# New planning constants for the last five attention blocks, and a later bank for output tiles, in a planned attention-and-MLP kernel

## The chip, the cores and the metric

The kernel runs on one core of a Trainium2 chip. The metric is the device time of one execution in microseconds (us), as the median of several runs; lower is better.

## The reference

One layer over S = 2048 positions with D = 448 channels. The input is normalized, and an attention with 16 heads of 28 channels and a two-layer MLP of width 1792 both read the normalized input. The MLP's result, through a silu, is a gate on the attention's projected output:

```python
xn = _layernorm(x)                      # x: (1, 2048, 448)
q, k, v = heads(xn @ wqkv)              # 16 heads of 28
p = softmax(q @ k.T * 28 ** -0.5)       # (2048 x 2048) per head
s = merge(p @ v) @ wo
g = silu(gelu(xn @ w1 + b1) @ w2 + b2)  # w1: 448 x 1792
return x + s * g
```

## The kernel before

**Tiling.** The heads form four groups of four (G = 4), the queries four chunks of 512 (C = 4). A group and a chunk make a block, so there are 16 blocks, done in the order of `ORD`; the last five, numbers 11 to 15, are (3,0), (3,1), (3,2), (2,3) and (3,3). A block has 64 score tiles of 128 keys by 512 queries, numbered m, one per key tile and head. TensorE (PE) computes the scores into banks of PSUM (`ring`, and `misc`; line L1429), ScalarE (ACT) takes the exponential of two or three tiles in one instruction (L1485), and PE multiplies the result with the values into the bank `acc` (L1865).

**Late passes.** ACT is relieved of some tiles. `p_late` picks groups of four tiles (one key tile, four heads) and VectorE (DVE) makes a rough exponential of them by integer arithmetic: four instructions that read PSUM (L1714, one per tile) and two that add a shift over all four (L1773). The product with the values then takes three sets of matmuls instead of one, or two where GpSimd (POOL) first adds two of them (L1786, four instructions). Only eight key tiles of a block may be picked (four in block 15), and only those at least `QDIST` tiles ahead of the next score.

**A block's end.** `p_epi` copies the sums and products of the block out of PSUM on DVE (L1928), and sends the sums through a chain: a DMA to DRAM and one back (L1940, L1942; block 14 has four direct DMAs instead, L1937), a reciprocal on POOL (L1944), a DMA to DRAM (L1946), four DMAs that spread the reciprocals over the partitions (L1949), and a product on POOL (L1953), after which the block's heads are ready for the output projection. All DMAs of this chain are issued by SyncE (SP). Block 15 ends in four parts (`p_epi4`, `p_norm4`): a copy (L1897), a matmul that spreads the sums (L1909), a reciprocal on DVE or, in the last part, on ACT (L1916, L1913), a product on DVE (L1919).

**Output.** For a query chunk c there are four output tiles t. `p_out` (c = 0, 1, 2) and `p_last` (c = 3) take a bank, project with four matmuls (L1963), multiply with the gate (`t_oev`: L1980 on DVE; at the very end for c = 2 a copy on ACT, L1976, and a product on DVE, L1978), add x (L1984) and store (L1986 on SP); for c = 0 and 1 a DMA from POOL accumulates into the output (L1989). The gate itself comes from f2, the second MLP matmul (L1346, evicted by L1352), a tanh on ACT (L1362), and then two POOL instructions per tile (L1367, L1369) for c = 0 to 2. For c = 3 two DVE instructions (L1373) make three tiles, the first two of them and the third alone.

**What sets the order.** The program is written by a planner: `run` steps through generators, one for each piece of work, each of which yields a task with an engine, what it reads and writes, a duration and a rank; the planner keeps a clock for each engine, takes the task that can start first by its own costs, with ranks deciding among those that start within `EPS`, and appends it to that engine's instruction list. The chip then runs each engine's list in that order, with semaphores between the engines. A wrong duration thus changes no result; it makes an engine stand at an instruction whose input is not there yet, with everything behind it. A generator that needs a PSUM bank asks for it with a condition; `p_out` asks when `on_done` of its block is set, its gate is done, and the product L1953 lies in the planner's past. Constants in `BP` are one row for each block; `tune` loads the row when the scores reach the block. Among them are `OP`, the rank of output tiles (a low one goes first; scores have 1, and products with the values 1.01 to 6), `QDIST`, `QLEAD`, `ND4`, `LU`, `LQ`, `JMAX` and `DQ`, which set when late passes are picked and how many may be under way, `MG` (whether POOL adds), `R3` (whether ACT may take three tiles at once), and `EPS`, `MP`, `SLACK`, `UR`, which bend the choice on PE.

Of the kernel before, what the change touches and what calls it, by code (L numbers as in the profile page):

```python
# [18 lines left out]
G = 4  # L19
# [7 lines left out]
NBLK = G * C  # L27
# [23 lines left out]
)  # L51
NQ = (5, 11, 13, 13, 12, 7, 11, 10, 16, 3, 16, 15, 12, 13, 12, 14)
# [12 lines left out]
R3, OP = 0, 5.0  # L65
# [25 lines left out]
PVN = 2  # L91
OWN2 = 0
EA = 0
LNR = 1
G3P = 0
PATH = {(1, 2): 'D', (1, 3): 'D', (2, 0): 'D', (2, 1): 'D', (2, 2): 'D', (2, 3): 'D'}
# [30 lines left out]
class _Kernel:  # L127
# [1229 lines left out]
    def p_silu(self, c):  # L1357
        K = self
        yield ("until", lambda: K.f2n[c] == 4 and K.ready([K.b_fsb[c % 2]], 0.3) and (c < 2 or K.g_done[c - 2]))
        fb, sg = K.fsb[:, c % 2, :, :], K.sig[:, c % 2, :, :]  # L1360
        nt = 4 if c < C - 1 else 3
        yield _Task(ACT, lambda eng: eng.activation(sg[:, 0:nt, :], fb[:, 0:nt, :], ACTF.Tanh, scale=0.5),  # L1362
                    [K.b_fsb[c % 2]], [K.b_sig[c % 2]], 0.1 + 0.375 * nt, 0.0, 0)
        if c < C - 1:
            for t in range(nt):
                o = K.g_sb[:, c, t, :]
                yield _Task(POOL, lambda eng, o=o, t=t: eng.tensor_tensor(o, sg[:, t, :], fb[:, t, :], ALU.mult),  # L1367
                            [K.b_sig[c % 2], K.b_fsb[c % 2]], [K.b_h[c], K.b_g[c]], 1.05, 0.05, 3, port=True)
                yield _Task(POOL, lambda eng, o=o, t=t: eng.tensor_tensor(o, o, fb[:, t, :], ALU.add),  # L1369
                            [K.b_sig[c % 2], K.b_fsb[c % 2]], [K.b_h[c], K.b_g[c]], 1.05, 0.05, 3, port=True)  # L1370
        for t0 in range(0, nt if c == C - 1 else 0, 2):
            t1 = min(t0 + 2, nt)
            yield _Task(DVE, lambda eng, t0=t0, t1=t1: eng.scalar_tensor_tensor(  # L1373
                K.g_sb[:, c, t0:t1, :], sg[:, t0:t1, :], 1.0, fb[:, t0:t1, :], op0=ALU.add, op1=ALU.mult),
                        [K.b_sig[c % 2], K.b_fsb[c % 2]], [K.b_h[c], K.b_g[c]], 0.15 + 0.467 * (t1 - t0), 0.0, 3)
        K.g_done[c] = True
        if c == C - 2:
            K.b_x2[c].r = list(K.b_h[c].r) + [K.b_h[c].w]
            for y in K.b_h[1], K.b_h[2]:
                K.b_x2[c].r += y.r + [y.w]  # L1380
            xc = K.A_x[0].rearrange("(c p t) d -> c p t d", p=128, t=4)[c]
            for i in range(OWN2 // 2, 2):
                dst = K.h[:, 1 + i, 5632:5632 + 2 * D].rearrange("p (t d) -> p t d", d=D)
                K.dma(SP, lambda eng, i=i, dst=dst: eng.dma_start(dst, xc[:, 2 * i:2 * i + 2, :]), K.s_x3, writes=[K.b_x2[c]] if i else [])
        if c < C - 1:
            return
        K.b_x2[c].r = list(K.b_h[c].r) + [K.b_h[c].w]
        K.dma(SP, lambda eng: eng.dma_start(K.x2[1][:, :, :], K.A_x[0].rearrange("(c p t) d -> c p t d", p=128, t=4)[c]),
              K.s_x2[c], writes=[K.b_x2[c]])
        if nt < 4:  # L1390
            yield ("until", lambda: K.exp_m == MTOT - 1)
            o = K.g_sb[:, c, 3, :]
            yield _Task(ACT, lambda eng: eng.activation(sg[:, 3, :], fb[:, 3, :], ACTF.Tanh, scale=0.5),
                        [K.b_fsb[c % 2]], [K.b_sig3], 0.47, 0.0, 0)
            if LNR:
                K.prog[ACT].append(lambda eng: eng.preload_act_table_set("natural_log_exp_and_others"))
                K.tE[ACT] += 1.3
            E = POOL if G3P else DVE
            if not G3P:
                yield ("until", lambda: K.E_done == NBLK + 1)  # L1400
            yield _Task(E, lambda eng: eng.tensor_tensor(o, sg[:, 3, :], fb[:, 3, :], ALU.mult),
                        [K.b_sig3, K.b_fsb[c % 2]], [K.b_h[c], K.b_g3a], 1.05 if G3P else 0.39, 0.0, 2, port=E == POOL)
            if not G3P:
                yield ("until", lambda: K.on4[3])
            yield _Task(E, lambda eng: eng.tensor_tensor(o, o, fb[:, 3, :], ALU.add),
                        [K.b_fsb[c % 2], K.b_g3a], [K.b_h[c], K.b_g3], 1.05 if G3P else 0.39, 0.0, 2, port=E == POOL)
# [481 lines left out]
    def p_epi4(self, s):  # L1888
# [3 lines left out]
        yield ("until", lambda: K.on_done[NBLK - 3])  # L1892
        if s == 2 and EA:
            yield _Task(ACT, lambda eng: eng.activation(K.E_sb[:, 1, sl], K.acc[:, sl], ACTF.Copy), [K.b_acc],
# [9 lines left out]
    def p_norm4(self, t):  # L1904
# [6 lines left out]
        R = K.rf[:, t % 2, :]  # L1911
        if LNR and t == 3:
            yield _Task(ACT, lambda eng: eng.activation(R, bank[:, 0:128], ACTF.Ln), [tok], [K.b_rf[t % 2]], 0.25, 0.0, 0)  # L1913
# [9 lines left out]
    def p_epi(self, b):  # L1923
        K = self
        g, c = ORD[b]
# [3 lines left out]
        K.E_done = b  # L1929
        K.copying = False  # L1930
        yield ("until", lambda: K.late_on)
        lag = 2.2 if b >= NBLK - 4 else 4.0
        src = bass.AP(tensor=K.E_sb, offset=DH * 1024 + 512 * (b % 2), ap=[[32 * 1024, 4], [1, 512]])
        if b == NBLK - 2:
            for j in range(4):
# [57 lines left out]
    
    def p_out(self, c, t):
        K = self
        bank, tok = yield ("bank", lambda: K.pe_free() and K.on_done[11 + c] and K.g_done[c] and K.ready(K.b_onT[G - 1][c:c + 1]), lambda: OP)
        K.pe_wait += 1
        ps = bank[:, 0:D]
        yield K.t_wo(ps, tok, c, t, (0, 1), lambda: OP)
        yield K.t_wo(ps, tok, c, t, (2, 3), lambda: OP)  # L2000
        K.pe_wait -= 1
        yield from K.t_oev(ps, tok, c, t)
        K.banks.append((bank, tok))
# [63 lines left out]
```

## Time and profile before

| | |
|---|---|
| median of 3 runs | 421.41 us (421.1 to 421.66) |
| the profiled execution, whole | 421.52 us |
| its span in the profile | 419.7 us |
| ACT busy | 406.0 us, 97% |
| PE busy | 400.8 us, 95% |
| DVE busy | 344.6 us, 82% |
| POOL busy | 186.3 us, 44% |
| DMA queues | 15.29 MB moved, mean 36 GB/s |

The span is what the hardware profiler records on the core; 1.8 us of the execution lie outside it. A profile's busy time counts work and not waits between engines. PE's matmuls are pipelined and their ends are modelled, so PE's busy share is not its share of full speed. Ends of the last blocks, by the copy L1928: block 10 at 302.4 us, 11 at 325.9, 12 at 343.4, 13 at 370.8, 14 at 389.6; block 15's first part is copied (L1897) at 405.4 us.

### The profile page before, as it was taken

The page shows a single profiled execution, that of the slowest core. Times are in us where ns is not written, and L with a number is a line of the kernel's source. Part 1 is how long each engine was busy: PE and PEld are TensorE (multiplying, and loading weights), DVE is VectorE, ACT ScalarE, POOL GpSimd, SP SyncE. Part 2 cuts the span into 40 slices and gives each one's busy share as a digit, 9 for nine tenths or more (in the row PEclk, how much of TensorE's full clock was granted, in tenths as well). Part 3 has the DMA queues.
Part 4 walks back from the last instruction along what each step waited for, and adds up shares of the span by engine and source line. Part 5 has one row for each costly group of instructions (what it writes and reads, how often), then busy time and mean ns, then how long its engine had stood idle before and what let it go on. Part 6 is the DMA issues. An engine that isn't in the chain of part 4 may idle for free.

```text
span 419.7 us, 9637 instructions
## 1 busy us (share of the span) xinstructions
PE 400.8 (95%) x3664; PEld 133.1 (32%) x3664; DVE 344.6 (82%) x594; ACT 406.0 (97%) x415; POOL 186.3 (44%) x193
## 2 busy tenths in 40 slices
PE   6899999999999999999999999999999999999995
PEld 4443223332222222223223433232223223222452
DVE  8968899987785899999893126799996899898577
ACT  6999999999999999999999999999999999999995
POOL 7571333237769271212331514408246805921860
PEclk9999999999999999999999999999999999999998
DMA  8801000000001001000220000000000012320032
GB/s 264 269 2 39 3 14 15 20 11 16 24 2 27 2 1 29 2 27 15 83 89 26 27 1 2 2 2 22 7 1 28 3 28 52 47 41 28 3 91 92
DMA packets 15952, 15.29 MB, mean 36 GB/s; under 512 B 7129, under 2 KB 12993, under 8 KB 15874
## 3 DMA queue, kind: packets, MB, share of 16 engines
q1 hardware_dynamic: 15042, 13.07, 10.8%
q0 software_dynamic: 576, 0.92, 1.6%
q8 instruction: 29, 0.48, 0.5%
q10 hardware_dynamic: 288, 0.69, 0.4%
q14 instruction: 17, 0.14, 0.1%
HBM read 12.59 MB, written 2.93 MB: 37 GB/s over the span
## 4 chain that ended last, share of the span: by engine, by line
PE 71%; ACT 12%; DVE 8%; issue 6%; POOL 2%; ACTq 0%; DVEq 0%; POOLq 0%
PE ring L1429 22%; PE acc L1865 17%; PE ring L1277 9%; ACT P L1485 7%; PE ring L1346 4%; PE misc L1346 4%; PE ring L922 3%; ACT h L1485 3%; PE misc L922 3%; PE misc L1277 2%; PE misc L1216 2%; DVE vaug L1714 1%; ACT xnT L1485 1%; PE acc L1063 1%; PE ring L1216 1%
## 5 line engine op out<-in xcount | busy, mean ns | idle before, releaser
L1485 ACT ACTIVATE P<-ring 128x1024 bf16<-128x1024 f32 (+1 forms) x237 | 251.1, 1163 | 3.0 <-PE ring L1429 1.3
L1429 PE MATMUL ring<-qT,kT 32*128 32x512 bf16 (+2 forms) x1060 | 141.6, 357 | 7.8 <-ACT P L1485 2.1
L1485 ACT ACTIVATE h<-ring 128x1024 bf16<-128x1024 f32 (+1 forms) x80 | 87.3, 1194 | 0.1
L1429 PEld LDWEIGHTS ring<-qT,kT 32*128 32x128 bf16 x1060 | 38.1, 91 | 144.1 <-ACT P L1485 83.9
L1944 POOL TENSOR_TENSOR rc<-rs,mone 128x16 f32<-128x16 bf16 x15 | 45.0, 3002 | 30.9 <-DMA rs<-sums 23.0
L1865 PE MATMUL acc<-P,vaug 128*32 128x512 bf16 (+2 forms) x607 | 54.0, 353 | 0.0
L1277 PE MATMUL ring<-xnT,w 128*128 128x512 bf16 x180 | 48.9, 382 | 0.0
L1485 ACT ACTIVATE xnT<-ring 128x1024 bf16<-128x1024 f32 (+1 forms) x40 | 44.2, 1144 | 1.0 <-PE ring L1429 0.6
L1953 POOL TENSOR_TENSOR qT<-x_sb,E_sb 128x512 bf16<-128x512 f32 x15 | 18.5, 1234 | 47.4 <-DVE w L1773 14.1
L1429 PE MATMUL misc<-qT,kT 32*128 32x512 bf16 (+1 forms) x92 | 34.6, 379 | 0.0
L1346 PE MATMUL ring<-w,h 128*128 128x448 bf16 x126 | 30.8, 355 | 0.3 <-DVE vaug L1714 0.3
L1714 DVE TENSOR_SCALAR x_sb<-ring 128x512 uint16<-128x512 f32 x43 | 29.0, 686 | 1.7 <-PE ring L1429 1.3
L1171 POOL TENSOR_TENSOR qsq<-qT 128x512 bf16<-128x512 bf16 x12 | 12.5, 1040 | 34.0 <-DVE qT L1165 31.4
L1865 PE MATMUL acc<-h,vaug 128*32 128x512 bf16 (+1 forms) x226 | 27.2, 380 | 0.0
L1714 DVE TENSOR_SCALAR x_sb<-misc 128x512 uint16<-128x512 f32 x29 | 19.9, 687 | 8.1 <-PE misc L1429 7.4
L1346 PE MATMUL misc<-w,h 128*128 128x448 bf16 x98 | 24.3, 356 | 0.0
L1277 PEld LDWEIGHTS ring<-xnT,w 128*128 128x128 bf16 x180 | 14.7, 97 | 23.9 <-issue 8.3
L1714 DVE TENSOR_SCALAR h<-ring 128x512 uint16<-128x512 f32 x31 | 21.1, 686 | 0.3 <-PE ring L1429 0.2
L1367 POOL TENSOR_TENSOR h<-w 128x448 bf16<-128x448 bf16 x12 | 12.7, 1059 | 18.4 <-DVE h L1773 14.5
L1865 PEld LDWEIGHTS acc<-P,vaug 128*32 128x32 bf16 x607 | 13.7, 95 | 15.8 <-issue 12.4
L1798 POOL TENSOR_SCALAR vs<-vaug 128x128 bf16<-128x128 bf16 x32 | 9.6, 299 | 20.6 <-DVE w L1773 18.0
L1261 DVE CAST h<-ring 128x512 bf16<-128x512 f32 x21 | 14.4, 686 | 4.4 <-PE ring L1277 4.3
(267 smaller groups left out, 699.0 us busy)
## 6 DMA issues: line engine op xcount, KB each, us to landing
x_sb<-recs SPq DMA_DIRECT2D x60, 64.0 KB, 2.0
w<-in_B_w_dram SPq DMA_DIRECT2D x1, 1568.0 KB, 7.3
w<-in_B_w_dram SPq DMA_DIRECT2D x1, 1344.0 KB, 8.5
x_sb<-in_A_x_dram SPq DMA_DIRECT2D x2, 448.0 KB, 5.6
out_dram<-in_A_x_dram SPq DMA_DIRECT2D x2, 448.0 KB, 10.3
out_dram<-h POOLq DMA_DIRECT2D x4, 224.0 KB, 4.2
out_dram<-h SPq DMA_DIRECT2D x8, 112.0 KB, 1.7
h<-in_A_wqkv_dram SPq DMA_DIRECT2D x3, 168.0 KB, 5.2
```

What stands on the lines that cost most here:

```text
L922: return eng.matmul(bank, w[:, k, g * 128:(g + 1) * 128], K.xnT[:, k, c * 512:(c + 1) * 512], start=(k == 0), stop=(k == KT - 1))
L1216: ins = eng.matmul(bank[:, off:off + nh * DH], K.xnT[:, kt, t * 128:(t + 1) * 128], ap, start=(kt == 0), stop=(kt == KT - 1), skip_group_c ...
L1261: yield _Task(DVE, lambda eng: eng.tensor_copy(dst, bank), [tok], wr, 0.69, 0.0, 2)
L1277: return eng.matmul(bank, K.w1[:, k, ft * 128:(ft + 1) * 128], K.xnT[:, k, c * 512:(c + 1) * 512], start=(k == 0), stop=(k == KT - 1))
L1346: ins = eng.matmul(ps, hv[:, ft, t * 128:(t + 1) * 128], K.w2[:, ft, :], start=(ft == 0), stop=(ft == FT - 1))
L1367: yield _Task(POOL, lambda eng, o=o, t=t: eng.tensor_tensor(o, sg[:, t, :], fb[:, t, :], ALU.mult), [K.b_sig[c % 2], K.b_fsb[c % 2]], [K.b ...
L1429: return eng.matmul(dst, K.kT[32 * j:32 * j + 32, g, t * 128:(t + 1) * 128], K.qT[32 * j:32 * j + 32, g, c * 512 + q0:c * 512 + q0 + nq], ...
L1485: return eng.activation(reg[:, i0:i0 + n, :], K.ring[:, b0:b0 + n, :], ACTF.Exp, scale=SM_SCALE)
L1714: yield _Task(DVE, lambda eng: eng.tensor_scalar(K.part(u, k).bitcast(dt.uint16), K.like(u, bank), SM_SCALE * LOG2E * 128.0, (127.0 - EXP_ ...
L1865: return eng.matmul(K.acc[32 * j:32 * j + 32, q0:q0 + nq], w, ap[:, col:col + nq] if len(ap.shape) == 2 else ap[:, col // 128:(col + nq) / ...
L1944: yield _Task(POOL, lambda eng: eng.tensor_tensor(K.rc[:, :], K.rs[:, :], K.mone[:, 0:1].to_broadcast([128, 16]), ALU.pow), [K.b_srs, K.b_ ...
L1953: yield _Task(POOL, lambda eng: eng.tensor_tensor(dst, K.rb, E, ALU.mult), [K.b_rb, tE], [K.b_onT[g][c]], 1.15, 0.05, 1, port=True)
```

## The change

Three things are changed. The rows of `BP` for blocks 11 to 15 get other constants. The planner counts a late DMA of blocks 12 to 14 as 3.0 us instead of 2.2, and the gate on DVE as 0.3 + 0.64 us per tile instead of 0.15 + 0.467. And an output tile asks for its bank only when its product L1953 lies 1.0 us back by the planner's clock, not at once. No instruction changes its form; the order of the instructions from block 11 on, the tiles that are picked for late passes there, and what POOL adds, come out of the planner anew. The planner's cost for the four spreading DMAs (L1949) is the same lag plus 0.6 us.

```diff
 # BP, rows 11 to 15, of
 # MG GQ GE EPS PV0 PVC MP ND4 LU JOINT LQ JMAX DQ URG SLACK UR QLEAD QDIST R3 OP
-(1, 0.227, 11, 0.189, 12, 6, 0.124, 6, 16, 0.113, 1, 6, 4, 8, 1.0, 1.3, 75, 24, 0, 2.977),
-(0, 5.612, 12, 0.1, 9, 2, 0.124, 4, 18, 0.375, 1, 4, 8, 2, 0.413, 0.922, 90, 16, 1, 5.0),
-(0, 4.459, 18, 0.121, 15, 10, 0.175, 5, 6, 0.039, 1, 5, 10, 3, 0.519, 1.838, 60, 34, 0, 3.491),
-(0, 2.463, 13, 0.143, 12, 3, 0.232, 9, 16, 0.053, 1, 5, 9, 12, 0.378, 1.28, 90, 16, 0, 5.0),
-(1, 4.0, 5, 0.1, 12, 7, 0.124, 3, 18, 0.132, 1, 3, 8, 5, 0.223, 0.491, 48, 20, 2, 5.0),
+(0, 0.227, 10, 0.102, 12, 6, 0.124, 9, 17, 0.113, 1, 6, 4, 8, 1.0, 1.3, 75, 28, 0, 3.77),
+(0, 5.612, 12, 0.137, 9, 10, 0.124, 4, 18, 0.4, 1, 4, 8, 2, 0.413, 1.275, 90, 16, 4, 5.0),
+(1, 6.265, 18, 0.121, 15, 2, 3.663, 5, 6, 0.064, 1, 3, 8, 3, 0.519, 2.119, 60, 38, 0, 3.491),
+(0, 2.077, 13, 0.119, 14, 3, 0.232, 9, 16, 0.334, 1, 1, 9, 12, 0.378, 1.28, 88, 16, 0, 6.0),
+(1, 4.0, 5, 0.1, 6, 6, 0.298, 3, 18, 0.206, 1, 3, 8, 21, 0.202, 0.491, 48, 20, 2, 1.109),
+LAG, ONS = 3.0, 1.0
 # p_silu, the gate of chunk 3 (t0 to t1 are one or two tiles)
-    [K.b_sig[c % 2], K.b_fsb[c % 2]], [K.b_h[c], K.b_g[c]], 0.15 + 0.467 * (t1 - t0), 0.0, 3)
+    [K.b_sig[c % 2], K.b_fsb[c % 2]], [K.b_h[c], K.b_g[c]], 0.3 + 0.64 * (t1 - t0), 0.0, 3)
 # p_epi
-    lag = 2.2 if b >= NBLK - 4 else 4.0
+    lag = LAG if b >= NBLK - 4 else 4.0
 # p_out
-    bank, tok = yield ("bank", lambda: K.pe_free() and K.on_done[11 + c] and K.g_done[c] and K.ready(K.b_onT[G - 1][c:c + 1]), lambda: OP)
+    bank, tok = yield ("bank", lambda: K.pe_free() and K.on_done[11 + c] and K.g_done[c] and K.ready(K.b_onT[G - 1][c:c + 1], -ONS), lambda: OP)
```

## The prediction

> **What bounds the kernel now.** I read the page's engine shares, then busy time by stretches from block 11 on, then the timeline around each stall.
>
> ```profile
> span 419.7 us, 9637 instructions
> PE 400.8 (95%) x3664; PEld 133.1 (32%) x3664; DVE 344.6 (82%) x594; ACT 406.0 (97%) x415; POOL 186.3 (44%) x193
> ```
>
> ACT is the bound. The stretches (length, then busy PE, PEld, DVE, ACT, POOL) show where it is not kept busy:
>
> ```profile
> 340.00:360.00 20.00, 19.93 (x193) 5.86 (x185) 19.35 (x33) 19.98 (x23) 9.11 (x8) 1.00 0.23 41
> 360.00:380.00 20.00, 18.09 (x144) 4.98 (x143) 18.66 (x29) 18.30 (x21) 10.28 (x8) 1.00 0.21 34
> 380.00:400.00 20.00, 19.86 (x294) 7.56 (x292) 13.16 (x21) 19.65 (x18) 10.96 (x8) 1.00 0.07 20
> 400.00:410.00 10.00, 8.84 (x222) 5.15 (x217) 8.60 (x15) 9.24 (x9) 5.33 (x5) 1.00 0.42 103
> ```
>
> ACT misses 1.70, 0.35 and 0.76 us in the last three; from 300 to 360 it misses 0.02. So at most 2.8 us of stalls can be removed in the changed stretch. DVE misses 6.84 us from 380 to 400. The first stall, in the timeline:
>
> ```profile
> 358.63 1.33 POOL L1367 TENSOR_TENSOR h<-w 128x448 bf16<-128x448 bf16 x1
> ...
> 359.63 1.44 POOL L1953 TENSOR_TENSOR qT<-x_sb,E_sb 128x512 bf16<-128x512 f32 x1
> ...
> 361.12 0.55 PE L1963 MATMUL ring<-wo,qT 128*128 128x448 bf16 x2 [0.95 <-POOL qT L1953]
> ...
> 361.61 0.39 PE L1429 MATMUL ring<-qT,kT 32*128 32x512 bf16 x3
> ...
> 362.05 6.53 ACT L1485 ACTIVATE P<-ring 128x1024 bf16<-128x1024 f32 x7 [0.97 <-PE ring L1429]
> ```
>
> An output tile of chunk 1 stands on PE before its product L1953 is done; the scores behind it are late and ACT stands 0.97 us. The second:
>
> ```profile
> 401.87 1.57 DVE L1373 SCALAR_TENSOR_TENSOR h<-w 128x896 bf16<-128x896 bf16 x1 [0.50 <-ACT w L1362]
> ...
> 403.90 1.04 DVE L1373 SCALAR_TENSOR_TENSOR h<-w 128x448 bf16<-128x448 bf16 x1
> ...
> 405.40 0.41 DVE L1897 CAST E_sb<-acc 128x256 bf16<-128x256 f32 x1
> ...
> 405.86 0.23 PE L1909 MATMUL ring<-E_sb,selb 128*128 128x128 bf16 x1 [0.83 <-DVE E_sb L1897]
> ...
> 407.12 1.03 ACT L1485 ACTIVATE P<-ring 128x1024 bf16<-128x1024 f32 x1 [0.76 <-PE acc L1865]
> ```
>
> The gate makes DVE late, the copy L1897 waits behind it, PE stands 0.83 us at L1909 with scores and value products queued behind, and ACT stands 0.76. Last, the tail. The last exponential starts at 410.27 and takes 1.04; the span goes on for 8.4 us. Of its end:
>
> ```profile
> 414.81 0.62 DVE L1980 TENSOR_TENSOR h<-ring,h 128x448 bf16<-128x448 f32 x1
> ...
> 415.34 0.55 ACT L1976 ACTIVATE h<-ring 128x448 bf16<-128x448 f32 x1 [0.40 <-PE ring L1963]
> ...
> 415.65 0.69 DVE L1984 TENSOR_TENSOR h<-h 128x448 bf16<-128x448 bf16 x2
> ...
> 416.68 0.39 DVE L1984 TENSOR_TENSOR h<-h 128x448 bf16<-128x448 bf16 x1
> ```
>
> L1976 is only for chunk 2. Two of chunk 2's tiles, whose product L1953 was done at 385.16 (384.00 + 1.16), are thus the last work of the kernel, after chunk 3's own.
>
> **The change part by part.** The sum is made against the profiled execution, 421.52 us (span 419.7 and 1.8 around it), 0.11 above the median.
>
> Later bank and longer lag. Block 12's chain has four DMA steps, each now 0.8 us longer by the planner, and the bank is asked for 1.0 us later: 4 x 0.8 + 1.0 = 4.2 us. The weight loads of L1963 waited 1.4 us for L1953, so this covers it three times over. The chain itself was not late by DMA here: POOL ran L1367 (1.33 us) ahead of L1953, and before that two issues of L1989 (1.12 and 0.88 us), for which the planner counts nothing on POOL. A delay of that kind could come back if L1953 is now put behind more gate work, each instruction 1.04 us; four would eat the margin. Gain between 0 and 0.97; I take 0.9. For block 14 the three steps from copy to spread reciprocals, without the reciprocal, took 390.33 to 394.02, 396.96 to 398.40, and 398.40 to 402.45 at most (POOL was busy until then): 3.7, 1.4, 4.1, in all 9.2, where the planner had 2.2 + 2.2 + 2.8 = 7.2 and now has 9.6. Block 13's four (371.53 to 373.13, to 374.72, 378.00 to 379.41, to 384.00) took 9.2, where it had 9.4 and now has 12.6. So the new lag is right for block 14 and too long for block 13: work after block 13 is planned some 3 us later than it could run. That is nothing for ACT, since chunk 2's tiles waited far longer than that anyhow.
>
> Gate. The planner's two instructions grow from 1.08 and 0.62 to 1.58 and 0.94 us, 0.82 in all, as the trace has (1.57, 1.04); and PE stood 0.83 at L1909. With the true time L1909 should be put behind the scores and value products. It gains between 0 and 0.76; another instruction may stand there, so I take 0.5. One row speaks against a fixed time: L1953 at 402.45 took 2.01 us, where its median is 1.16, beside these very gates, and POOL's L1786 (401.34, 1.15 us) ran beside the first. The Trainium skill ("SBUF — State Buffer", Who interferes with whom) says that a DVE instruction with two inputs in SBUF and a GpSimd instruction that reads SBUF exclude one another for the whole instruction. The trace agrees: the first gate would wait 0.62 us, to 402.49, and then take 0.95; L1953 would wait until 403.44 and take 1.02; the second gate would wait to 404.46 and take 0.48. By it the old costs were the true ones and the loss is a neighbour's; where POOL is idle the gate is 1.2 us shorter than planned, which leaves my 0.5 as it is, and with POOL beside it the cost holds.
>
> Rank of output tiles. In block 15 `OP` falls from 5 to 1.109, ahead of f2 and most value products. Six tiles (two of chunk 1, four of chunk 2) were made from 399.35 on; block 15's scores start at 384.96, and DVE is a third idle there. If chunk 2's tiles are gone by 410, chunk 3's last tile ends with L1980 at 415.43 and an L1984 of 0.38, at 415.81 instead of 417.07: 1.26 us. Gain 0 to 1.26; two tiles must both move, so I take 0.8. They cost PE four matmuls of 0.215 us each, 0.86 a tile. PE waits for ACT 35 us from 300 to 412 (27.5 and 7.6 in the waits of its score weights), which hides them; where one stands ahead of a late score, it costs ACT up to 0.86. I take 0.4 for all of them, 0 to 1.7.
>
> POOL's sums and the rest. `MG` off in block 11 removes one sum (309.89 to 317.26, four instructions) and adds a set of value matmuls, 0.215 us on PE under the same cover: nothing. `MG` on in block 13 is the reverse: POOL is idle half of that time; nothing, but L1953 could queue behind 4.6 us. `R3` 4 in block 12 lets ACT take more triples: two tiles take 0.92 us from start to start, three 1.33 (337.71 to 339.04), so three pairs made two triples save 3 x 0.92 - 2 x 1.33 = 0.1; with at most five such exchanges 0 to 0.5, taken as 0. The other constants (`EPS`, `MP`, `SLACK`, `UR`, the ranks of value products, `OP` 3.77 and 6 in blocks 11 and 14) bend the order and change no instruction; what a bad order costs is a stall like the two above, 0.8 to 1.0 us, and what a good one may still save is ACT's other idle time, 2.8 - 0.97 - 0.76 = 1.1 us. I take 0 between these ends.
>
> Late passes. A group takes four tiles off ACT, 4 x 0.461 = 1.85 us (eight pairs from 301.71 to 309.09), and puts six instructions 0.60 apart on DVE, 3.6 us. The trace has 71 instructions of L1714 after 302.4, about 18 groups, of 36 allowed. `QDIST` grows by 4 in blocks 11 and 13 (fewer picks), `ND4` from 6 to 9 and a freer DVE allow more. The diff does not tell the count; I take none gained or lost, with one either way, 1.85, as the bound.
>
> Sum: -0.9 - 0.5 - 0.8 + 0.4 = -1.8, or 419.7 profiled; 419.6 as a median.
>
> **The rivals.**
>
> - Fewer late passes, slower. Two groups less in blocks 11 and 13, through `QDIST` 28 and 38, put 3.7 us on ACT against 1.8 gained: 423.3. It decides from the second lost group on; one leaves 421.5. For it: a tile must be picked earlier, and DVE was 97% busy from 340 to 360. Against: 18 of 36 is far from a cap, so other limits (buffers) may rule.
> - Tiles crowd the tail, slower. Lag and the 1.0 us push tiles back; with two more behind the last exponential each costs DVE two instructions of 0.38 (L1978, L1984) and waits, about 1 us: 419.6 + 0.8 (the gain not had) + 2 = 422.4. Against: rank 1.109.
> - One group more on an idle DVE: 419.6 - 1.85 = 417.8. For it: 15.8 us of idle DVE from 300 to 410; against: only 7 L1714 ran from 380 to 400, where it idles most.
> - Nothing gained: stalls go and others come, since PE runs in order and every block is laid anew: 421.4.
>
> **How the numbers follow.** What measurement tells from no change is about 0.2%, 0.84 us. Forecast (418.5 to 420.5) 0.47, one group more 0.12, nothing gained 0.14, fewer groups 0.15, crowded tail 0.12. Faster 0.47 + 0.12 = 0.59, same 0.14, slower 0.27. The range runs from 417.6, below one group more, to 422.6, above the crowded tail; it leaves out most of the lost groups. The forecast's own range stands above.
>
> **What would show it.** Right: no wait of L1963 for L1953 over 0.3 us; ACT idle from 300 to the last exponential below 1.8 us; no L1976, or L1976 not last; 66 to 76 instructions of L1714 after block 10's copy. Wrong: L1714 count outside that, more than two tiles of chunk 2 after the last exponential, or a new stall of ACT over 0.8 us, at a matmul that stands before its input.

## The result and the profile after

The changed kernel takes 420.69 us (median of 16 runs, 420.18 to 421.54), the kernel before 421.46 us in the same session (16 runs). The ratio is 0.9979, with a 95% interval of 0.9971 to 0.9987: 0.9 us faster, between 0.5 and 1.2 us. The prediction had the direction, and the time lies in its whole range (417.6 to 422.6), just above the forecast's own (418.5 to 420.5); it promised 1.8 us and half of that came. The profiled execution takes 420.68 us instead of 421.52.

The changed file has one line more, so a line of the changed kernel has a number one higher from there on: L1429 is L1430, L1963 is L1964, and so on. In the engine shares of its page, ACT is still the bound, and PE, DVE and ACT do nearly the same work as before:

```profile
span 418.9 us, 9607 instructions
PE 396.6 (95%) x3640; PEld 133.8 (32%) x3666; DVE 345.0 (82%) x594; ACT 404.8 (97%) x412; POOL 188.2 (45%) x193
```

The count of late passes has not moved: 70 instructions L1715 start after block 10's copy, where before has 69 of L1714 (the prediction's 71 counts some twice that cross the edge of a window), and from block 9's sums on ACT takes 268 score tiles in both kernels. The stretches of the changed kernel (length, then busy PE, PEld, DVE, ACT, POOL, granted clock, DMA share, GB/s):

```profile
340.00:360.00 20.00, 19.11 (x153) 5.49 (x154) 19.09 (x30) 19.03 (x21) 12.68 (x10) 1.00 0.25 38
360.00:380.00 20.00, 19.75 (x165) 5.86 (x160) 18.06 (x30) 19.89 (x22) 15.09 (x13) 1.00 0.11 32
380.00:400.00 20.00, 19.75 (x314) 7.76 (x312) 12.57 (x20) 19.96 (x17) 9.99 (x6) 1.00 0.06 9
400.00:410.00 10.00, 9.09 (x160) 4.44 (x154) 8.72 (x17) 8.58 (x9) 4.43 (x4) 1.00 0.61 143
```

Read the ACT column against the same stretches of before: it now misses 0.97 us where it missed 0.02, then 0.11 instead of 1.70, 0.04 instead of 0.35, and 1.42 instead of 0.76. The two stalls that the prediction showed, at 361 and at 407, are gone. Others stand in their place. From 300 to the last exponential ACT misses 2.54 us, where it missed 2.83.

The largest new stall, in the timeline of the changed kernel (start, duration, then the instruction; in brackets the idle time before it and what ended that):

```profile
395.53 2.91 POOL L1945 TENSOR_TENSOR rc<-rs,mone 128x16 f32<-128x16 bf16 x1 [1.85 <-DMA rs<-E_sb]
...
398.41 3.10 POOL L1787 TENSOR_TENSOR wk<-wk,xnT 128x512 bf16<-128x512 bf16 x2
...
398.87 1.64 DVE L1374 SCALAR_TENSOR_TENSOR h<-w 128x896 bf16<-128x896 bf16 x1 [0.47 <-ACT w L1363]
...
400.97 1.04 DVE L1374 SCALAR_TENSOR_TENSOR h<-w 128x448 bf16<-128x448 bf16 x1
...
401.66 0.40 PE L1866 MATMUL acc<-wk,vs 128*32 128x256 bf16 x8 [0.91 <-POOL wk L1787]
```

PE stands 0.91 us at value products whose sum L1787 is not ready, and ACT's next exponential is 0.92 us late, at 402.93. The cause is further up: POOL's two sums are queued behind the reciprocal L1945, and that waited for the last of block 14's four DMAs (L1938), which the planner counts as 3.0 us. From the copy's end at 390.68 it took 4.85, to 395.53. The chain of work that ended last runs through the same instructions (start, duration, what):

```profile
395.53 2.91 POOL rc L1945
398.44 3.09 POOL wk L1787 x2
401.53 0.14 issue
401.66 0.40 PE acc L1866 x8
```

So where did the 0.8 us of the profiled executions come from? Block 9's sums are sent at 277.85 before and at 278.05 after, a difference that the start of the kernel brings. From there to the end of the last exponential it is 133.46 us before (411.31) and 133.45 after (411.50), although ACT idles a little less. From the last exponential to the end of the span it is 8.39 before and 7.40 after. The whole gain lies behind the last exponential. There the gate comes 3.0 us earlier (398.87, before 401.87), L1977 (before L1976), the copy of chunk 2's tiles on ACT, is no longer run, and DVE has less left to do. Stretches from the end of the last exponential to the end of DVE's last instruction, first before, then after:

```profile
411.31:417.07 5.76, 3.99 (x51) 1.93 (x49) 5.49 (x16) 3.43 (x7) 0.00 (x0) 1.00 0.27 89
```

```profile
411.50:416.70 5.20, 3.26 (x69) 1.67 (x57) 5.17 (x14) 2.35 (x5) 0.00 (x0) 1.00 0.23 76
```

DVE (third pair of columns) is busy 5.49 of 5.76 and 5.17 of 5.20 us. In these two kernels it bounds this stretch: the end is the last exponential plus what DVE still has to do, plus 2.1 to 2.6 us for the last store.

### The profile page after: what moved, and what is told of

Same layout as the page of the kernel before. It is cut to its first block, busy times and chain, and to the rows that moved or that the text cites. A ratio compares the mean times of both kernels' runs of the same rounds, so it can differ in the third digit from the quotient of the medians.

```text
span 418.9 us, 9607 instructions
## 1 busy us (share of the span) xinstructions
PE 396.6 (95%) x3640; PEld 133.8 (32%) x3666; DVE 345.0 (82%) x594; ACT 404.8 (97%) x412; POOL 188.2 (45%) x193
## 4 chain that ended last, share of the span: by engine, by line
PE 60%; ACT 23%; issue 8%; DVE 6%; POOL 2%; ACTq 0%; POOLq 0%; DVEq 0%
PE ring L1430 18%; PE acc L1866 13%; ACT P L1486 13%; PE ring L1278 8%; ACT h L1486 7%; PE ring L1347 7%; PE ring L923 2%; PE misc L923 2%; PE misc L1347 2%; ACT xnT L1486 2%; PE misc L1278 1%; PE ring L1217 1%; PE acc L1064 1%; PE misc L1217 1%; PE ring L1964 1%
## 5 line engine op out<-in xcount | busy, mean ns | idle before, releaser
L1430 PE MATMUL ring<-qT,kT 32*128 32x512 bf16 (+2 forms) x1045 | 140.9, 357 | 9.7 <-ACT P L1486 2.0
L1430 PEld LDWEIGHTS ring<-qT,kT 32*128 32x128 bf16 x1045 | 38.0, 91 | 144.0 <-ACT P L1486 81.0
L1945 POOL TENSOR_TENSOR rc<-rs,mone 128x16 f32<-128x16 bf16 x15 | 45.0, 2997 | 32.7 <-DMA rs<-sums 24.5
L1278 PE MATMUL ring<-xnT,w 128*128 128x512 bf16 x169 | 46.0, 381 | 1.4 <-issue 0.8
L1486 ACT ACTIVATE xnT<-ring 128x1024 bf16<-128x1024 f32 (+2 forms) x38 | 43.0, 1172 | 2.0 <-PE ring L1430 1.4
L1954 POOL TENSOR_TENSOR qT<-x_sb,E_sb 128x512 bf16<-128x512 f32 x15 | 19.6, 1304 | 51.9 <-PE acc L1866 21.2
L1347 PE MATMUL ring<-w,h 128*128 128x448 bf16 x168 | 40.5, 355 | 0.3 <-DVE vaug L1715 0.3
L1430 PE MATMUL misc<-qT,kT 32*128 32x512 bf16 (+1 forms) x107 | 40.7, 382 | 0.0
L1866 PE MATMUL acc<-h,vaug 128*32 128x512 bf16 x230 | 27.9, 384 | 0.0
L1715 DVE TENSOR_SCALAR x_sb<-ring 128x512 uint16<-128x512 f32 x38 | 25.7, 685 | 1.7 <-PE ring L1430 1.3
L1715 DVE TENSOR_SCALAR x_sb<-misc 128x512 uint16<-128x512 f32 x30 | 20.6, 686 | 4.7 <-PE misc L1430 4.0
L1715 DVE TENSOR_SCALAR h<-ring 128x512 uint16<-128x512 f32 x33 | 22.3, 685 | 0.0
L1347 PEld LDWEIGHTS ring<-w,h 128*128 128x128 bf16 x168 | 12.3, 97 | 17.9 <-issue 10.6
```

What stands on the lines that cost most here:

```text
L1278: return eng.matmul(bank, K.w1[:, k, ft * 128:(ft + 1) * 128], K.xnT[:, k, c * 512:(c + 1) * 512], start=(k == 0), stop=(k == KT - 1))
L1347: ins = eng.matmul(ps, hv[:, ft, t * 128:(t + 1) * 128], K.w2[:, ft, :], start=(ft == 0), stop=(ft == FT - 1))
L1430: return eng.matmul(dst, K.kT[32 * j:32 * j + 32, g, t * 128:(t + 1) * 128], K.qT[32 * j:32 * j + 32, g, c * 512 + q0:c * 512 + q0 + nq], ...
L1486: return eng.activation(reg[:, i0:i0 + n, :], K.ring[:, b0:b0 + n, :], ACTF.Exp, scale=SM_SCALE)
L1715: yield _Task(DVE, lambda eng: eng.tensor_scalar(K.part(u, k).bitcast(dt.uint16), K.like(u, bank), SM_SCALE * LOG2E * 128.0, (127.0 - EXP_ ...
L1866: return eng.matmul(K.acc[32 * j:32 * j + 32, q0:q0 + nq], w, ap[:, col:col + nq] if len(ap.shape) == 2 else ap[:, col // 128:(col + nq) / ...
```

## The experiments

Twelve kernels were run. The table has their times, each ratio (of mean times) against runs of the kernel before on the same chip, and from the profiled execution the end of the last exponential, what DVE worked from there to its last instruction, and the span. In the profiled executions of e1 and e12 the granted clock of PE fell to 0.50 for 3.41 us near the end, so their last three columns hold what that cost as well.

| kernel | median us | ratio to before (95%) | last exp ends | DVE left | span |
|---|---|---|---|---|---|
| before | 421.46 | | 411.31 | 5.49 | 419.7 |
| changed | 420.69 | 0.9979 (0.9971 to 0.9987) | 411.50 | 5.17 | 418.9 |
| e1, rank put back | 422.0 | 1.0021 (1.0006 to 1.0036) | 412.56 | 6.68 | 421.7 |
| e2, rank alone | 422.62 | 1.0024 (1.0014 to 1.0034) | 411.23 | 7.18 | 420.8 |
| e3, gate alone | 422.04 | 1.0013 (1.0004 to 1.0021) | 410.35 | 6.72 | 419.9 |
| e4, longer transfer | 419.76 | 0.9957 (0.9945 to 0.9969) | 410.26 | 5.31 | 417.8 |
| e5, terms without rows | 424.04 | 1.0065 (1.0050 to 1.0079) | 413.86 | 5.11 | 421.4 |
| e6, rows without terms | 422.62 | 1.0029 (1.0019 to 1.0039) | 411.57 | 6.89 | 420.8 |
| e7, bank alone | 425.74 | 1.0095 (1.0081 to 1.0109) | 415.54 | 2.76 | 422.2 |
| e8, e4 with the old gate cost | 420.43 | 0.9974 (0.9963 to 0.9984) | 409.68 | 6.52 | 418.5 |
| e9, no POOL sum in block 15 | 420.79 | 0.9991 (0.9978 to 1.0003) | 410.22 | 5.59 | 418.9 |
| e10, row 15 put back | 420.61 | 0.9981 (0.9971 to 0.9990) | 410.00 | 5.81 | 418.7 |
| e11, e4 with the rank put back | 420.68 | 0.9980 (0.9972 to 0.9989) | 409.26 | 6.68 | 418.4 |
| e12, e4 with row 15 put back | 421.74 | 1.0017 (1.0000 to 1.0033) | 414.72 | 4.35 | 423.1 |

### One stall and what it costs (e4, e9)

e4 is the changed kernel with one duration longer: the planner counts block 14's four DMAs as 4.8 us.

```diff
 # p_epi, the four direct DMAs of block 14
-    reads=[tE], writes=[K.b_srs] if j == 3 else [], land=max(K.now, tE.tw) + lag)
+    reads=[tE], writes=[K.b_srs] if j == 3 else [], land=max(K.now, tE.tw) + 4.8)
```

> The changed kernel with 4.8 instead of 3.0 us counted for the four DMAs of block 14's sums (4.85 us from the end of the copy to the reciprocal in the trace of the changed kernel). Only POOL's order changes: its four sums L1787 now stand ahead of the reciprocal instead of two behind it. Theory C (the new stall of ACT, 0.92 us at 402.9, comes from those two sums standing behind a reciprocal that waits 1.85 us for its DMA): stall gone, PE no longer waits 0.91 us for L1787, time 0.6 to 0.9 us lower, about 420.0. Rival (the sums were late by the gate beside them, or the end is set by DVE's output work): 420.7 within 0.3.

The orders of PE, DVE, ACT and SP are the same; on POOL the four sums now stand ahead of the reciprocal. It measured 419.76 us (five runs, 419.24 to 420.20), 0.9957 of before, the fastest kernel of this study. Timeline of e4:

```profile
391.14 4.49 POOL L1787 TENSOR_TENSOR wk<-wk,xnT 128x512 bf16<-128x512 bf16 x4 [1.50 <-DVE xnT L1774]
395.61 2.90 POOL L1945 TENSOR_TENSOR rc<-rs,mone 128x16 f32<-128x16 bf16 x1
...
398.59 1.09 DVE L1374 SCALAR_TENSOR_TENSOR h<-w 128x896 bf16<-128x896 bf16 x1 [0.46 <-ACT w L1363]
...
400.13 0.61 DVE L1374 SCALAR_TENSOR_TENSOR h<-w 128x448 bf16<-128x448 bf16 x1
```

The reciprocal starts at 395.61, 0.08 us later than in the changed kernel, so the sums run almost wholly in time that POOL spent waiting. PE waits no longer, and ACT works through from 400 to 405. The last exponential ends 1.24 us earlier, of which 0.29 is there before the stall (an exponential starts at 394.55, in the changed kernel at 394.84), so 0.95 is left; the ratios differ by 0.0022, or 0.9 us. The stall of 0.92 at 402.93 cost its whole length. The second reading is the gate: with no sum of POOL beside it, it takes 1.09 and 0.61 us, not 1.64 and 1.04.

e9 takes the same stall away by another route: in block 15 POOL adds nothing.

```diff
 # BP, row 15, MG
-(1, 4.0, 5, ...
+(0, 4.0, 5, ...
```

> The changed kernel with `MG` 0 in block 15, so that POOL adds nothing there and the value products that stood at 401.66 behind POOL's L1787 (3.10 us, queued behind the reciprocal L1945) no longer wait for POOL; PE gets one set of matmuls L1866 more instead. Theory (the stall of 0.92 us at 402.93 is POOL's queue behind a transfer that the planner counts too short, and it delays the end): the stall goes by this way too, the last exponential ends about 410.6 instead of 411.50, and the median is 419.8 to 420.1, near the 419.76 of the kernel with the longer transfer. Rival 1 (DVE alone sets the end, the kernel with the longer transfer won by another order on DVE): the stall goes and the median stays at 420.5 to 420.9. Rival 2 (the planner, laid anew, puts another stall there): a stall over 0.8 us elsewhere after 395 and 421 or more.

The stall went (ACT works 5.00 of 5.00 us from 400 to 405, and the last exponential ends at 410.22), and yet the median was 420.79: the theory missed, and the first rival's time came out. What the earlier last exponential gave was given back behind it: one tile of chunk 2 ends on ACT again (L1977), and the last DVE instruction ends 6.32 us after the last exponential instead of 5.20. In e9, from there on:

```profile
410.22:416.54 6.32, 3.57 (x78) 2.02 (x78) 5.59 (x15) 2.76 (x5) 0.00 (x0) 1.00 0.22 69
```

DVE's work grew by 0.42 us (5.59 after 5.17) and its waiting by 0.70. So a stall of ACT is worth its length only where what follows the last exponential, DVE's work and its waits, does not grow with it, as in e4.

### The gate's cost alone (e3)

```diff
 # before, p_silu
-    ... [K.b_h[c], K.b_g[c]], 0.15 + 0.467 * (t1 - t0), 0.0, 3)
+    ... [K.b_h[c], K.b_g[c]], 0.3 + 0.64 * (t1 - t0), 0.0, 3)
```

> The kernel before with the gate's cost alone at 0.3 + 0.64 per tile; only the last rows of PE, DVE and ACT differ. The prediction's step (L1909 is put behind scores and value products, and ACT's stall of 0.76 us at 407.1 goes): about 420.9. Rival (another instruction stands there, or the tail takes the time back since DVE is as busy as before): 421.4 within 0.3.

The stall at 407 is gone: ACT works 5.91 of the 6 us from 405 to 411, and the last exponential ends 0.96 us earlier than before, 0.28 of which is there already at the gate (401.59, before 401.87). That leaves 0.7, about the stall of 0.76. The time is 0.13% longer all the same, 422.04 us, above both forecasts. From the last exponential to DVE's last instruction, in e3:

```profile
410.35:417.37 7.02, 4.01 (x51) 1.84 (x49) 6.72 (x19) 3.42 (x7) 0.00 (x0) 0.98 0.18 58
```

It has 6.72 us left to do where it had 5.49. The exponentials came early; what must follow them on DVE did not. This is the point where the prediction's step for the gate fails: its stall goes as forecast, and is worth nothing.

### The bank alone (e7)

```diff
 # before, p_out
-    K.ready(K.b_onT[G - 1][c:c + 1]), lambda: OP)
+    K.ready(K.b_onT[G - 1][c:c + 1], -1.0), lambda: OP)
```

> The kernel before with the bank of output tiles asked for 1.0 us later, nothing else. The prediction's step: L1963 waits no more for L1953 at 361, ACT's 0.97 us is gone, about 420.5. Theory A: that stall goes, ACT's idle time from 300 to the last exponential falls by less than 0.5 because others come, and the end, set by VectorE after the gate, stays: 421.4 within 0.5.

The first stall goes here too: from 360 to 380 ACT works 19.93 of 20 us, before 18.30. But the kernel is 0.95% slower, 4 us, far above both forecasts, and 2.5 us slower in the profiled execution, which is the shortest of its six runs (423.99; the others 425.71 to 425.96, and no trace shows what they did). Its timeline has ACT idle 1.43 us at 391.88, 0.72 at 401.79, 0.92 at 403.73 and 1.87 at 414.02. In the middle lie POOL's sums and the gate:

```profile
394.46 5.33 POOL L1786 TENSOR_TENSOR kT<-kT,vaug 128x512 bf16<-128x512 bf16 x4
...
396.83 3.44 DVE L1373 SCALAR_TENSOR_TENSOR h<-w 128x896 bf16<-128x896 bf16 x2 [1.15 <-ACT w L1362]
```

The two instructions of the gate take 3.44 us together beside the sums; alone they take 1.70 (e4). The output tiles behind the gate are late, and PE stands at L1963. One thing more is different: 65 instructions L1714 start after block 10's copy instead of 69, and ACT takes 272 score tiles from block 9's sums on instead of 268. This kernel has lost one group of late passes, which at the prediction's 0.461 us a tile is an estimated 1.8 us on ACT. So e7 does not price the later bank by itself.

### Terms without rows, rows without terms (e5, e6)

```diff
 # e5: the rows of BP as before; the late transfer 3.0, the gate's cost and the 1.0 us of the bank as changed
 # e6: the rows of BP as changed, and
-LAG, ONS = 3.0, 1.0
+LAG, ONS = 2.2, 0.0
-    0.3 + 0.64 * (t1 - t0)
+    0.15 + 0.467 * (t1 - t0)
```

> The rows of before with all three new planner terms (lag 3.0, gate 0.3 + 0.64, bank 1.0 us later); PE changes from block 12's end on. The prediction's steps: the stalls of 0.97 and 0.76 us go, about 420.1. Theory A: stalls are exchanged and the end is set by VectorE's output work behind the gate, so without rows that bring the gate and block 15's first part earlier than 401.9 and 405.4 the time stays at 421.4 or gets worse, up to 422.5.

> The rows of after with the old terms (lag 2.2, gate 0.15 + 0.467, bank at once). Theory A: the rows bring the gate 3 us earlier whatever the terms, so the tail keeps most of its gain, and where an output tile stands before its product a stall of about 1 us comes back: 420.7 to 421.7. Rival (the terms carry the gain): 421.4 or more, gate not before 401.

Each half of the change is slower than before, e5 by 0.65%, more than was expected, and e6 by 0.29%, with the rival's late gate. In e5 the stall at 361 is gone (ACT 20.00 of 20 us from 360 to 380), and the gate starts at 396.36, 5.5 us earlier than before. Then one sum of four instructions on POOL, spread from 399.09 to 406.9 between a product and two accumulating DMAs, holds the value products, and with them the buffers of the exponentials:

```profile
405.16 1.75 POOL L1786 TENSOR_TENSOR vaug<-vaug,wq 128x512 bf16<-128x512 bf16 x1
```

```profile
409.23 1.45 ACT L1485 ACTIVATE xnT<-ring 128x1536 bf16<-128x1536 f32 x1 [4.97 <-PE acc L1865]
```

In e6 the gate is late, at 405.37. So it is the terms that bring it forward in the changed kernel, the later bank above all (396.83 in e7, 401.59 with the gate's cost alone in e3), and the rows that keep this from ending in a stall like that of e5.

### The rank of output tiles (e2, e1, e11)

```diff
 # e2: before, with row 15 ending in
-... 48, 20, 2, 5.0),
+... 48, 20, 2, 1.109),
 # e1: changed, and e11: e4, with row 15 ending in
-... 48, 20, 2, 1.109),
+... 48, 20, 2, 5.0),
```

> The kernel before with OP of block 15 alone at 1.109; only the last rows of PE, DVE and ACT differ. Theory A: tail shorter by 0.7 to 1.0 us, the stalls of 0.97 and 0.76 us stay: about 420.6. Rival B: 421.4 within 0.3. If the six tiles ahead of the scores cost ACT more than the tail gains: 421.7 or more.

In e2 L1976 disappears as the prediction's step said, and the last exponential ends where it did. But DVE has 7.18 us left instead of 5.49, and the time is 0.24% longer, as the last of the three expectations had it:

```profile
411.23:418.66 7.43, 3.75 (x48) 1.59 (x47) 7.18 (x18) 2.34 (x5) 0.00 (x0) 0.89 0.20 65
```

With the low rank, output tiles go ahead of the first L1909, which falls from 405.86 to 409.46, and three reciprocals L1916 that before were spread start at 409.73, 411.58 and 412.59.

> The changed kernel with OP of block 15 put back from 1.109 to 5.0; PE, DVE and ACT differ from the changed kernel only in their last 50 or so rows, POOL and SP not at all. Theory A (the whole gain is the tail: chunk 2's output tiles no longer come after the last exponential, while ACT's stalls were only exchanged): tiles of chunk 2 end by way of L1976 again, the stretch from the last exponential to the end goes from 7.4 back to about 8.4 us, and the time from 420.7 to about 421.4. Rival B (the gain is in the stalls that went, and the tail is set by DVE whatever the rank): 420.7 within 0.3.

e1 is 1.3 us slower than the changed kernel, and L1977 stands three times at the end. That alone would price the rank at 1.3 us, but ACT also has stalls of 1.88 us at 403.47 and 1.19 at 407.02 there. For the first, POOL's sums took longer still. Timeline of e1:

```profile
398.46 1.09 DVE L1374 SCALAR_TENSOR_TENSOR h<-w 128x896 bf16<-128x896 bf16 x1 [0.47 <-ACT w L1363]
398.49 3.57 POOL L1787 TENSOR_TENSOR wk<-wk,xnT 128x512 bf16<-128x512 bf16 x2
...
400.00 1.05 DVE L1374 SCALAR_TENSOR_TENSOR h<-w 128x448 bf16<-128x448 bf16 x1
```

The second has another cause. PE stood idle for 1.87 us, until 402.21, and from 403.74 to 407.15 its granted clock was 0.50. In that stretch the projection L1964 took 0.95 us instead of 0.55, and the scores before the exponential at 407.02 took 0.97. The last two lines are stretches (length, busy ACT, granted clock, DMA share, GB/s):

```profile
402.21 0.40 PE L1866 MATMUL acc<-wk,vs 128*32 128x256 bf16 x8 [1.87 <-POOL wk L1787]
402.54 0.55 PE L1964 MATMUL misc<-wo,qT 128*128 128x448 bf16 x2
...
405.48 0.95 PE L1964 MATMUL misc<-wo,qT 128*128 128x448 bf16 x2
...
406.37 0.97 PE L1430 MATMUL ring<-qT,kT 32*128 32x128 bf16 x24
```

```profile
400.00:405.00 5.00, 3.12 (x4) 0.87 0.58 163
405.00:411.00 6.00, 4.82 (x5) 0.82 0.47 67
```

Not every run of e1 had this. Five of the twelve took 423.25 to 423.84 us, with a mean granted clock of 0.994 to 0.996 (the profiled one among them), the other seven 421.31 to 422.08, at 0.998 or more, with a median of 421.76. Without the lower clock e1 is thus 1.1 us slower than the changed kernel.

e11 separates rank and stall: it has e1's order on every engine but POOL, where the sums stand ahead of the reciprocal.

> The kernel with the longer transfer (block 14's four DMAs counted as 4.8 us, 419.76) with `OP` of block 15 back at 5.0. Against the kernel with the rank alone put back (422.0) it differs only in POOL's list: four sums L1787 stand together ahead of the reciprocal L1945. So it prices the rank without the stall, and the stall without the rank. Theory (the end is the last exponential plus what DVE still has to do; the stalls of 1.88 and 1.19 in the run with the rank put back came from POOL's sums of 3.57 us): the stall at 403 goes, the last exponential ends at 410.0 to 410.6 instead of 412.56, chunk 2's tiles (L1977) lie in the tail, DVE has 6.2 to 7.0 us left instead of 5.34, and the median is 420.5 to 421.0: the rank is worth 0.7 to 1.2 us, the stall about 1.2. Rival (the rank is worth the 1.3 us that the other pair of runs gave, and more where no stall hides it): 421.2 to 422. Rival 2 (the rank is worth nothing without the stall): 419.5 to 420.1.

420.68 us, as the theory had it, though with the last exponential 0.7 us earlier than it said. Against e1 (1.0021), which differs in POOL's list alone, the ratio of 0.9980 is 1.7 us better, 1.3 by the medians, and 1.1 against the median of e1's seven runs without the lower clock: that is about the price of the first stall, and the rest is what the lower clock cost. Against e4 (0.9957), which differs in the rank, it is 1.0 us worse by the ratios and 0.9 by the medians: the price of the rank in this order. From the last exponential on, e11:

```profile
409.26:416.25 6.99, 5.30 (x56) 2.40 (x54) 6.68 (x19) 3.96 (x8) 0.00 (x0) 1.00 0.26 85
```

Without the low rank the exponentials are done at 409.26, a full 1.0 us before those of e4, and DVE then has 6.68 us to do instead of 5.31. The low rank moves work from behind the last exponential to ahead of it: 1.0 us paid on ACT (0.14 of it is there already at block 9's sums), 1.6 saved behind it (9.14 to 7.54 from the last exponential to the end of the span), 0.6 net in the spans.

### Row 15, and the gate's cost once more (e10, e12, e8)

```diff
 # e10: changed, and e12: e4, with row 15 as before
-(1, 4.0, 5, 0.1, 6, 6, 0.298, 3, 18, 0.206, 1, 3, 8, 21, 0.202, 0.491, 48, 20, 2, 1.109),
+(1, 4.0, 5, 0.1, 12, 7, 0.124, 3, 18, 0.132, 1, 3, 8, 5, 0.223, 0.491, 48, 20, 2, 5.0),
```

> The changed kernel with the whole row of block 15 as before, `OP` 5 among it; rows 11 to 14 and the three terms as changed. Theory (the terms, by way of the earlier end of block 13, bring the gate forward, and row 15 only has to use it): the gate's first instruction still starts before 400.5, chunk 2's tiles end with L1977 behind the last exponential again, tail 9 us or more, median 421.8 to 422.6, as with the rank alone put back (422.0). Rival (row 15's other constants bring the gate forward): the gate starts at 402 or later, as before, and the median is 422.5 to 425.

The gate starts at 398.95, before 400.5, as the theory had it, so row 15 is not what brings it forward. The median, 420.61, is that of the changed kernel and 1.2 us better than the theory's range: a miss. In this order POOL's four sums happen to stand ahead of the reciprocal, so there is no stall at 403 and the gate takes 1.09 and 0.62 us. The last exponential ends at 410.00, 1.5 us earlier than in the changed kernel, the tail is 8.7 us instead of 7.4, and 6.16 us go by to DVE's last instruction instead of 5.20, with L1977 three times among the last work:

```profile
410.00:416.16 6.16, 4.55 (x53) 2.01 (x50) 5.81 (x16) 3.96 (x8) 0.00 (x0) 1.00 0.28 94
```

No stall and a long tail, or a stall and a short tail, give the same time.

> The kernel with the longer transfer (419.76) with the whole row of block 15 as before. Against the changed kernel with row 15 put back (420.61), where POOL's sums already stood ahead of the reciprocal, only the order of the last output tiles differs. Theory (no stall of ACT near the end, L1977 in the tail, DVE 6 us or more behind the last exponential): last exponential at 410.0 to 410.4, median 420.3 to 421.0. Rival (the longer transfer wins by something else than POOL's order, so it gains its 0.9 here too): 419.4 to 420.0.

421.74 us, outside both forecasts. The profiled execution was one of the two slowest of twelve (424.87), and in it the spread reciprocals came late: their first DMA was issued at 400.53, the product that needs them started at 407.98, 7.45 us later; in e10 that took 4.91. PE stood 2.30 us at L1964 for it, and ACT stood idle for 4.62:

```profile
407.98 1.15 POOL L1954 TENSOR_TENSOR qT<-x_sb,E_sb 128x512 bf16<-128x512 f32 x1 [3.59 <-DMA x_sb<-recs]
```

Here too the granted clock fell to 0.50, from 408.83 near the end of PE's idle time to 412.25, and five projections took 2.03 us where four take 0.93 at the full clock:

```profile
409.19 1.30 PE L1964 MATMUL ring<-wo,qT 128*128 128x448 bf16 x3 [2.30 <-POOL qT L1954]
...
410.39 2.03 PE L1964 MATMUL ring<-wo,qT 128*128 128x448 bf16 x5
```

That explains this execution, and probably the other of the two (424.31), which has a mean granted clock of 0.996. The other ten, from 421.17 to 422.26, make the median; no trace shows one of them, and their cause is open.

e8 is e4 with the gate's old cost, 1.08 and 0.62 us, which is what e4 measured for it.

```diff
 # e4, p_silu
-    0.3 + 0.64 * (t1 - t0)
+    0.15 + 0.467 * (t1 - t0)
```

> The kernel of e4_rs_lag with the gate's old cost, 0.15 + 0.467 per tile. In the trace of e4_rs_lag no POOL instruction runs beside the gate, and it took 1.09 and 0.61 us, the old costs (1.08, 0.62). If a true cost makes a good order: 419.3 to 419.8. If the longer cost helps because it puts output work later on VectorE, as a margin: 420.2 or more. POOL, SP and PE up to block 15's parts stay as they are.

420.43 us, as the second expectation had it, 0.7 us slower than e4 although its duration is the right one there. ACT has no stall over 0.1 us from 400 to 410 (9.93 of 10.00) and ends at 409.68, the earliest but e11; DVE has 6.52 us left. A truer cost made a worse order. That the planner fills ACT first while DVE ends last fits this, but no run tests it.

## Why the prediction was right in direction and wrong in size

**Late passes and the path outside the last 40 us**: right. The count stayed (70 after 69, and 268 tiles on ACT in both).

**Later bank and longer lag, 0.9 us.** The stall at 361 goes as described, with the bank alone (e7), with all terms (e5), and in the changed kernel. The gain was not there. PE serves a tight list for ACT, and the newly laid list has its own waits: 0.38 us at 351.92 for value products, 0.53 at 357.14 for scores, beside a late-pass instruction L1774 of 1.81 us (its usual duration is 0.68) that runs next to POOL's L1787. One reading in the prediction's working on the lag was too long: the steps of 4.6 and 4.1 us from the spreading DMAs to the product were 3.3 us of transfer each (379.41 to 382.71, 398.40 to 401.67); after that block 14's product stood behind other work of POOL, and block 13's waited for PE.

**Gate, 0.5 us.** The stall at 407 goes (e3), but it is worth nothing on its own (e3 is 0.13% slower), since what ends the kernel there is DVE. The prediction called ACT the bound and read each of its stalls as time at the end. The chain it should have followed is the one behind the last exponential, where DVE was busy 5.49 of 5.76 us.

**Rank, 0.8 us, less 0.4 for what it costs.** Right in kind in one pair of kernels: the rank is worth 0.6 us in the spans of e11 and e4 and 0.9 in their medians, and there both sides were too small: 1.6 us saved behind the last exponential, 1.0 paid ahead of it. It is no property of the rank: in the kernel before the same constant costs 0.24% (e2), and with all of row 15 put back, the rank too, the changed kernel takes the same time (e10). The measured tail of the change is 0.99 us shorter.

**The step that failed** is "I take 0 between these ends" for the other constants and for what a newly laid order costs. The prediction wrote that a bad order costs a stall of 0.8 to 1.0 us and that a good one may save 1.1, and then took neither. From 340 to 410 ACT got rid of 2.66 us of idle time (1.59 from 360 to 380, 0.31 from 380 to 400, the 0.76 at 407), more than the sum had for it, and took on 2.37 new (0.95 from 340 to 360, 1.42 from 400 to 410). The rival "stalls go and others come" describes this; the forecast's rank describes what the tail did. The largest new stall, 0.92 us at 402.93, is the missing half of the forecast: e4 removes it by POOL's list alone and reaches 0.9957, 1.8 us below before (1.3 to 2.3). From block 9's sums to the last exponential e4 takes 132.50 us (before 133.46), and its tail is 0.85 us shorter: close to the two parts of the sum, 0.9 + 0.5 - 0.4 on ACT and 0.8 in the tail. That the parts fit so well is in part luck, since the idle times that went and came are not only those that were named.

Adding up parts is what this step stands for, and the runs show it does not hold here. Of the three parts to which the prediction gave a gain, none gains alone: the bank is 0.95% slower (e7, with a group of late passes lost), the gate's cost 0.13% (e3), the rank 0.24% (e2). The direction of the whole came from an order that the prediction did not work out.

**The named marks.** The wait for L1953 and L1976 were gone, and L1714 was in its range. ACT's idle time was 2.54 us, above the 1.8 of the forecast, and there was a new stall over 0.8 at a matmul that stands before its input: the mark of a wrong prediction, as it was written.

**The gate's two costs.** The prediction had set the measured 1.57 and 1.04 us beside a rule by which the old costs, 1.08 and 0.62, were the true ones. The Trainium skill ("SBUF — State Buffer", Who interferes with whom) says that a DVE instruction with two inputs in SBUF and a GpSimd instruction that reads SBUF exclude one another, and that the order of issue decides which of them waits. The runs agree: the gate alone takes 1.09 and 0.61 (e4); where POOL's sum starts first, at 398.41, the gate at 398.87 takes 1.64 (changed); where the gate starts first, at 398.46, it takes 1.09, and the two sums take 3.57 instead of 2.26 (e1). The new constant, which fits the 1.57 and 1.04 us of before, is thus a duration with its neighbour in it. The prediction put the gate without a neighbour at 1.2 us below the new cost; alone it takes 1.70 where the cost is 2.52, so it is 0.8. The new cost helps the order all the same (e4 against e8), by way of what it delays, not because it is true.

## What to carry to other kernels

In this kernel a stall of the busiest engine was worth its length only where the engine that works after it had no more left to do in the end: look at who is busy behind the last instruction of the bound, and price each stall by what it does to that engine's remaining work. Where a planner lays a list anew, take the idle time that is left in the stretch as a term of its own, likely to be spent again, instead of adding up the stalls that are seen to go. A duration measured beside a neighbour belongs to the pair; look for the same instruction somewhere it runs alone before it goes into a cost.

## What was not expected of the hardware

The sums on POOL (L1787) take 2.26 us for two where DVE runs nothing against them, 3.10 and 3.57 beside the gate. The product L1954 takes 1.16 us in the median and 3.26 at 386.67 in the changed kernel. From the end of the copy to the use of the four small DMAs of the sums, which SP issues one behind another, it took 4.85 us in the changed kernel (from the first issue to the use 3.7 us before); of the four that spread the reciprocals, from the first issue to the use, 4.91 us in e10, 6.42 in e11 (399.82 to 406.24) and 7.45 in e12. The same four had landed 3.3 us after the first issue in before (398.40 to 401.67) and 3.2 in the changed kernel (399.91 to 403.15); what makes them slow in the others is open. Such a chain has no one duration, and a planner that stakes an in-order engine on it can lose the difference.

PE's granted clock is not given for good. PE stood idle for 1.87 us in e1 and for 2.30 in e12, and the clock was 0.50 for 3.41 us from 1.5 us after the end of the idle time in e1 (403.74) and from 0.4 before it in e12 (408.83). Two projections took 0.95 us in it instead of 0.55. After 0.95 us of idle time in before, 1.21 in e7 and 1.68 in e5 the profiled executions show no fall before the last work of the kernel. What sets its start these runs do not show. A stall that reaches PE can thus cost more than its length: in e1 the runs with the lower clock took 1.2 to 2.5 us more than those without.
